# A new list of steps for a one-core kernel that mixes a state-space layer with linear attention

## The chip, the cores and the metric

The kernel runs on one core of a Trainium2 chip. A core has a matrix engine (TensorE; PE in the profile, its weight loads PEld), a vector engine (VectorE; DVE), a scalar engine (ScalarE; ACT), GpSimd (POOL) and a sync engine (SyncE; SP) that here only issues DMAs. Each engine has its own queue of instructions and takes them in the order in which the program lists them; between engines, semaphores hold an instruction back until its data is there. The metric is the device time of one execution in microseconds (us), the median of several runs.

## The reference, cut to what matters

`x` is 2048 tokens of 512 features in bf16. Two branches read it, and a sigmoid gate mixes them:

```python
g = sigmoid((x * gate_w).sum(-1, keepdims=True))
# branch A: a complex diagonal recurrence over 2048 time steps
Lam_bar = exp(dt * Lam);  B_bar = ((Lam_bar - 1) / Lam)[:, None] * Bmat
Bu = einsum("bld,pd->blp", x, B_bar)
for t in range(L):  h = Lam_bar * h + Bu[:, t, :]
a = 2 * einsum("blp,dp->bld", hseq, Cmat).real + x * Dskip
# branch B: linear attention, 32 heads of 16, softmax(+p) and softmax(-p) as features
q, k, v = split(x @ wqkv);  pq, pk = q @ w_phi, k @ w_phi
phi = concat([softmax(p), softmax(-p)])          # for q and for k
kv = einsum("bhsf,bhsd->bhfd", phi_k, v);  z = phi_k.sum over s
o = (phi_q @ kv) / (phi_q @ z + 1e-6);  b = o @ wo
return g * a + (1 - g) * b
```

## The kernel before

All of `x` is held transposed in SBUF (`xT`), as 16 blocks of 128 tokens, regrouped so that tokens with the same remainder modulo 8 stand together. Branch B computes keys (steps `k0` to `k15`), values (`v0` to `v15`) and queries (`q0` to `q15`), each four matmuls into one PSUM bank and a copy out of it; features by maximum, minimum, exponential and sum (`x`, `n`, `e`, `s` with the number of a key group; `X`, `N`, `E`, `S` with the number of a query group of four blocks); and the sum of keys times values (`a`). Branch A makes the inputs of the recurrence for 8 groups of 64 complex states (`b` and `g` with group and part), runs a scan over every eighth step (`z0`, `z1`, each for half of the groups), and fills in the steps between (`sa`, `sb`, `H`, then `hd`, `hk`, `ek` on ACT, DVE and DMA and `dp` on PE). The output of block n is gathered in one PSUM bank: `yn` (branch A), `tn` (branch B times `wo`), with `on` making the normalized attention rows before that.

All of this is written as Python generators, one per step name, each yielding after a few instructions of one engine. The string `ORDER` lists the names; each time a name comes, its generator advances by one part:

```python
for tok in ORDER.split():
    tok, _, banks = tok.partition("@")
    tok, _, eng = tok.partition(":")
    sel["eng"] = "dve" if eng == "D" else "act"
    sel["banks"] = [int(b) for b in banks]
    next(st[tok])
```

So `ORDER` decides four things: the sequence of every engine's queue (program order is queue order), the PSUM bank that a step uses (`@3`: bank 3; `o` takes the named bank and the next one, as pairs), whether a copy out of PSUM or a scaling goes to DVE (`:D`) or to ACT, and the sequence of the DMAs. Nothing is planned at run time. Below, "part 2 of `z0`" means its third yield, counted from zero.

Parts that matter below:

- Loads on SP: `Lk` (two halves of the key weights), `Lx` (two plain loads of blocks 0 and 1, then seven DMA transposes of two blocks each, line 236; the last three bring blocks 10/11, 12/13 and 14/15), `Lv` (value weights), `Lq` (two DMA transposes of the query weights, line 249), `Lb` (two plain loads of `A_B_re` and `A_B_im`, line 241, then four DMA transposes to `BT`, line 244), `Lc` (four transposes of C, line 255), `Lo` (`wo`), `Ld` (the row `Dskip`, then two loads of 256 KB of `x` for the blocks whose skip term is added by DVE, line 272). Key block n needs its `Lx`; the query weights `w0` to `w3` need both `Lq`; `b` and `g` need `BT`.
- Other DMAs on SP: `C` (line 698), `XX0`, `XX1` (swapped halves of the states, line 774), the last two parts of each `S` (feature transposes, line 620), `O` (transposes of a pair of `on` rows, line 904, which `t` needs), `R` (output, line 932). A DMA that has to wait holds up everything behind it in SP's queue.
- `Z`: a matmul on zeros, sixteen of them at the head. `W`, `T`: PE transposes of weights and of blocks 0 and 1, each with a copy. `f0` to `f3`: the folded key weights.
- `a4` adds the last key group; `Y` (four parts on DVE, lines 829 and 831) masks the finished sums into `KVm`; every `o` reads `KVm`.
- `sb1`, `H2`, `H3`: one PE part and then an addition on DVE (line 735).
- part 3 of `on` is the normalization on DVE (line 891), which also frees the two banks of `on`.
- part 0 of a feature sum (`S1`: line 566, `sm<-EE`) reads what both exponentials of that group (line 589) have written.
- part 3 of `ekm` is the last addition on DVE for states of group m (line 806); part 0 of `y10` reads groups 0 to 3.

Of the kernel before, what the change touches and what calls it, by code (L numbers as in the profile page):

```python
# [23 lines left out]
ORDER = """
Z@0 Lk Lk Z Z Z B Z Z B Z Z Z Lx Z Z W01@2 Z W00@3 Z B Z W00 Z B W01 W10@1 W00 Lx B W10:D W11@4 Lx W01 Z f0@2 f1@5
T1@1 W11 T0@4 f0:D f1 Lv T1 f2@3 f3@0 Lx Lx T0:D f2 V@2 V k1@5 P k0@4 f3:D P Lx P2 P k0 P2 P2 U P2 k1 P2 U P3 P4 k0
k1 U k2@2 P3 P4 k3@1 n0 v0@5 P4 x0 k5@6 k2 v1@2 Lb Lq n0 i x0 P2 k7@0 v3@4 i V2@3 k3 x0 v0 k5 i n0 i k9@1 x0 v1 i i
Lq x0 n0 Lb k7 M n0 k8@7 k4@0 M k6@2 n1 M Lx w2@6 x1 w0@5 V2 v6@3 x0z Lx n1 x1 v3 n1 L Da Lx Lb Lb x1 Lb Da Lb e0 n1
k4 w3@4 k6 k9 w3 x1 w0 x1 v6 k10@0 n1 k10 s0 x2 k11@2 s0 w1@4 k8 M2 e1 k13@1 k15@3 w1 Db x2 k15 b11@7 U x2 b10@5 k11
b01@0 b20@4 n2 x2 Lc n2 b10 x2 n2 s0 w2 n2 M2 s0 k13 b00@3 n2 M2 g01@5 Da Db x3 g10@1 b30@6 s0 b01 b20 s0 Lc e2 Db  # L30
s1 b31@4 g10 g30@0 n3 b30 s0 c1:D x3 b00 g00@3 s1 g30 k12@6 c0:D b31 g00 g01 k14@2 e2 b11 a0@74 g00 gw a0 g01 g10 n3
q1@1 s1 b21@3 n3 x3 s1 Da s1 x3 g30 v2@0 c0:D k12 n3 s1 q3@6 k14 q0@2 g01 s2 x3 n3 s2 q1 q1 b21 Lc c0:D q2@3 n4
g11@1 x4 e3 g11 g11 q3 v2 g31@0 g01 s1 x4 q3 g20@6 g31 q0 q0 a1 q2 n4 s2 x4 e3 g31 g20 c0 g11 g01 n4 c2 g01 g31 a1
g01 g20 s2 g21@2 x4 q2 g11 s3 Lc g21 c2 g21 g11 s2 v5@3 g01 g21 c1 v5 g31 g21 s2 x4 v4@6 g21 s3 c2:D g31 s3 b40@3
g01 g11 v4 g21 n4 s3 g31 g21 s3 g31 v7@5 b50@6 b40 g21 g31 n4 g11 s2 q6@3 X0 N0 G0 c1 g21 s2 X0 g11 a2 q4@2 c2 g31
q7@0 c1 g11 q6 N0 b50 z0@6 c3 Lo z0 b70@1 v7 a2 q4 s3 z0 q4 q5@5 q7 a2 e4 q6 s3 q7 b70 q5 X0 e4 N0 z0 a2 c3 X0 b71@3
z0 g40@6 X0 b61@1 N0 z0@0 b71 g50@2 b61 g50 g50 q5 z0 z0 b51@5 X1 c3 v10@0 g40 s4 b60@3 z0 sa0@2 g70@1 b51 g61@5 N0
X1 b60 g71@3 s4 g71 g70 v10 g51@0 c3 sa0 X1 g40 sb0@2 Ld s4 s3 N1 g60@6 sb0 N1 s4 g51 g61 g51 N1 E0 E0 C g60 C g70
g51 S0 v11@2 s4 G1 N1 G0 v8@1 g60 Ld S0 g51 H1@6 g61 v11 s4 v8 X1 S0 b41@2 v9@1 g51 H1 S0 s4 hd1 C g51 s4 a3 S0 g71
v9 g41@6 a3 b41 g41 H0@2 g41 a3 a3 hd1 G0 g71 g51 C S0 g71 g61 g41 G1 S0 g71 g61 H0 g41 XX0 g41 q9@2 g61 g71 hd0 G1  # L40
g51 g51 g61 g71 g41 g61 q10@1 X1 g61 XX0 g41 N1 q9 g71 g41 g61 q8@0 g71 g41 S0 hd1 z1@6 q8 q10 z1 S0 z1 q11@3 q9 q11
v13@6 z1 q10 E1 q8 E1 z1 v12@0 XX0 z1@1 X2 N2 v14@2 q14@5 v13 q11 v12 z1 z1 X2 XX0 v15@1 N2 q12@3 z1 v15 hd0 v14 S0
S0 N2 hd1 hd1 hd0 hd1 q14 S1 a4 N2 S1 X2 sa1@0 a4 S1 sa1 a4 q12 a4 sb1@6 S1 q13@0 Y Y sb1 S1 hd0 q15@7 Y X2 H2@6 Y
o0@1 q14 G2 S1 END q15 X2 XX1 y1@5 q15 hd0 q13 q12 S1 o0 o1@3 H3@7 N2 y1 H3 o1 H2 hd0 o3@6 XX1 XX1 o0 q13 o0 o1 E2
E2 o1 N3 S1 XX1 y3@0 hk4 S1 o2@1 y2@4 y0@3 y2 O0 o2 y0 S1 y0 S2 o3 X3 o2 hk6 y1 o3 hk4 hk7 o2 t1 t0 y3 o3 hk7 hk6
y4@1 y2 S2 hk4 hk5 O1 t0 S2 o5@6 X3 S2 y3 hk4 hk7 S2 N3 t1 X3 S1 o4@2 S2 y6@5 hk5 X3 t2 S2 o5 ek0 hk5 hk7 R0 S2 o4
o5 o4 ek0 t3 hk5 hk6 t2 o4 ek3 ek3 o5 t3 o6@2 S2 N3 S2 hk6 X3 N3 o6 o7@6 y5@4 ek0 o7 o6 N3 o6 O2 o7 o7 ek2 ek1 y5 y4
y6 S2 dp5@0 ek1 y4 ek3 y5 dp6@2 o8@6 dp6 dp5 y6 E3 t4 ek2 Ld o9@2 o8 ek0 y7@0 o9 y7 ek2 ek1 o8 t5 o8 o9 ek2 o9 ek1
ek4:D E3 o10@6 t4 y7 o10 O3 o11@2 ek5 S3 t7 ek3 o10 t6 ek6 o11 ek4 o11 O4 y10@1 o10 S3 G2 dp1@6 ek5:D y11@7 t6 t7 t5
o11 ek5 S3 O5 ek7 ek6 ek4 ek5 ek7 S3 dp0@2 ek6 R2 ek7 ek4 y9@0 ek6 ek7 S3 dp7@4 y8@3 dp2@5 S3 dp2 y10 y8 dp3@5 t8  # L50
y11 S3 R1 S3 dp7 dp4@4 G2 dp1 u8 S3 S3 S3 t11 t8 G3 dp0 t10 y9 t9 o13@2 dp3 o13 o12@5 o12 u9 dp4 t9 R3 y14@4 y12@0
u10 o12 G3 y14 o12 o13 o15@5 o13 o15 y12 o15 o14@2 t10 o14 G3 y12 o14 u11 o15 y13@1 O6 y13 t11 y15@56 y15 y13 t12
t13 R4 R5 o14 O7 y14 t14 O8 t12 t13 R6 y15 t14:D R7 t15 t15 t15 R8 t15:D R8
"""
# [946 lines left out]
```

## Time and profile before

| | before |
|---|---|
| median of 3 runs | 151.49 us (151.43 to 152.28) |
| the profiled execution | 151.96 us, of which 150.2 us are the span from first to last instruction |
| granted TensorE clock | 0.996 |
| HBM read and written | 3.56 MB, 2.10 MB |
| DMA traffic in all | 19.73 MB, 131 GB/s on average |

The profile shows for each engine its busy time and its share of the span, and gives idle time to the event that ended it. A timeline line reads: start, duration, engine, source line, operation, output<-input, and in brackets the idle time before it and what ended that. Durations of neighbouring instructions overlap by 0.06 to 0.2 us, since an engine starts one before the last has drained; so the distance from start to start is the true price of a line, and the chain of waits prints such distances.

### The profile page before, as it was taken

The page shows a single profiled execution, that of the slowest core. Times are in us where ns is not written, and L with a number is a line of the kernel's source. Part 1 is how long each engine was busy: PE and PEld are TensorE (multiplying, and loading weights), DVE is VectorE, ACT ScalarE, POOL GpSimd, SP SyncE. Part 2 cuts the span into 40 slices and gives each one's busy share as a digit, 9 for nine tenths or more (in the row PEclk, how much of TensorE's full clock was granted, in tenths as well). Part 3 has the DMA queues.
Part 4 walks back from the last instruction along what each step waited for, and adds up shares of the span by engine and source line. Part 5 has one row for each costly group of instructions (what it writes and reads, how often), then busy time and mean ns, then how long its engine had stood idle before and what let it go on. Part 6 is the DMA issues. An engine that isn't in the chain of part 4 may idle for free.

```text
span 150.2 us, 2835 instructions
## 1 busy us (share of the span) xinstructions
PE 140.9 (94%) x986; PEld 75.2 (50%) x986; DVE 135.1 (90%) x332; ACT 121.9 (81%) x241; POOL 21.4 (14%) x47
## 2 busy tenths in 40 slices
...
GB/s 120 237 265 178 143 230 232 166 180 238 20 0 0 0 0 4 2 0 105 244 74 94 183 142 70 175 186 181 229 181 166 156 65 212 128 214 77 201 82 72
DMA packets 54110, 19.73 MB, mean 131 GB/s; under 512 B 44496, under 2 KB 54096, under 8 KB 54096
## 3 DMA queue, kind: packets, MB, share of 16 engines
...
q8 instruction: 7, 0.11, 0.3%
q14 instruction: 7, 0.06, 0.2%
HBM read 3.56 MB, written 2.10 MB: 38 GB/s over the span
## 4 chain that ended last, share of the span: by engine, by line
PE 55%; DVE 24%; SPq 10%; DMA 7%; issue 1%; ACT 0%; DVEq 0%
PE PS L516 12%; PE PS L860 9%; PE PS L648 9%; PE PS L643 9%; PE PS L916 6%; SPq L236 5%; DMA xT<-in_A_x_dram 4%; DVE on L891 3%; DVE sm L566 3%; SPq L249 3%; DMA oT<-on 3%; PE PS L660 2%; DVE EE L577 2%; DVE EE L616 2%; DVE HH L735 2%; DVE EE L583 2%
## 5 line engine op out<-in xcount | busy, mean ns | idle before, releaser
L516 PE MATMUL PS<-WKV,xT 128*128 128x480 bf16 (+1 forms) x128 | 29.6, 373 | 1.7 <-DMA xT<-in_A_x_dram 1.7
L589 ACT ACTIVATE EE<-EE 128x2048 bf16<-128x2048 bf16 x16 | 30.7, 1944 | 0.0
L516 PEld LDWEIGHTS <-xT 128*128 128x128 bf16 x192 | 18.3, 99 | 20.0 <-DMA xT<-in_A_x_dram 1.8
L860 PE MATMUL PS<-C,LS 128*128 128x512 bf16 (+1 forms) x104 | 23.0, 363 | 0.0
L135 ACT CAST Xq<-PS 128x480 bf16<-128x480 f32 x32 | 17.6, 584 | 1.7 <-PE PS L516 1.7
L916 PE MATMUL PS<-Wo,oT 128*128 128x512 bf16 (+2 forms) x68 | 15.6, 367 | 0.3 <-DMA oT<-on 0.3
L643 PE MATMUL PS<-xT,BT 128*128 128x512 bf16 x64 | 15.7, 379 | 0.0
L648 PE MATMUL PS<-xT,BT 128*128 128x512 bf16 x64 | 15.6, 379 | 0.0
L516 PE MATMUL PS<-Wq,xT 128*128 128x481 bf16 x64 | 15.0, 367 | 0.0
L135 ACT CAST LS<-PS 128x512 bf16<-128x512 f32 x24 | 14.1, 630 | 0.9 <-PE PS L648 0.7
L860 PEld LDWEIGHTS <-LS 128*128 128x128 bf16 x104 | 9.5, 98 | 9.7
L684 POOL DMA_DIRECT2D LS<-CT x4 | 4.9, 1226 | 62.2 <-ACT HH L135 49.6
L922 ACT ACTIVATE ot<-PS,G 128x512 bf16<-128x512 f32 (+1 forms) x11 | 7.2, 670 | 5.8 <-PE PS L916 5.7
L882 ACT ACTIVATE ld<-PS 128x32 f32<-128x32 f32 x16 | 2.8, 197 | 10.2 <-PE PS L877 7.6
L465 ACT ACTIVATE CT<-HH,dgs 128x512 bf16<-128x512 bf16 x15 | 10.7, 718 | 0.2 <-DVE HH L735 0.2
L891 DVE TENSOR_TENSOR on<-PS,rd 128x512 bf16<-128x512 f32 x16 | 10.8, 710 | 0.0
L577 DVE TENSOR_TENSOR EE<-Xq,mx 128x2048 bf16<-128x2048 bf16 (+1 forms) x9 | 10.0, 1107 | 0.8 <-PE PS L633 0.8
L465 ACT ACTIVATE CT<-CS,nsn 128x512 bf16<-128x512 bf16 x15 | 10.5, 725 | 0.0
L583 DVE TENSOR_TENSOR EE<-mn,Xq 128x2048 bf16<-128x2048 bf16 (+1 forms) x9 | 10.0, 1112 | 0.0
L566 DVE TENSOR_TENSOR sm<-EE 128x2048 bf16<-128x2048 bf16 (+1 forms) x9 | 10.0, 1107 | 0.0
L135 ACT CAST vx<-PS 128x512 bf16<-128x512 f32 x16 | 9.9, 633 | 0.1
L604 DVE TENSOR_TENSOR EE<-EE,rc 128x2048 bf16<-128x2048 bf16 x8 | 9.7, 1219 | 0.1
...
## 6 DMA issues: line engine op xcount, KB each, us to landing
...
```

Source lines behind the costliest of these rows:

```text
L135: nc.scalar.copy(out=out_ap, in_=in_ap)
L465: nc.scalar.mul(out=out_ap, in_=in_ap, mul=s_)
L516: MM(out=pt[:], lhsT=xT[:, kt, ti * P:(ti + 1) * P], rhs=W[:, kt, 0:pt.shape[-1]], start=(kt == 0), stop=(kt == KT - 1))
L566: VT(out=dst, in0=cur[:, :, :, 0:n, :], in1=cur[:, :, :, n:2 * n, :], op=op)
L577: VT(out=half(EE, 0), in0=X5, in1=live["mx", p].to_broadcast([P, L, 8, Dh, 4]), op=ALU.subtract)
L583: VT(out=half(live["EE", p], 1), in0=live["mn", p].to_broadcast([P, L, 8, Dh, 4]), in1=X5, op=ALU.subtract)
L589: aexp(out=EE[:, l_:l_ + 2], in_=EE[:, l_:l_ + 2], func=ACT.Exp)
L643: MM(out=pt[:], lhsT=BT[:, m, kt, :], rhs=cells(kt, r), start=(kt == 0), stop=False, skip_group_check=True)
L648: MM(out=pb[:], lhsT=BT[:, m, kt, :], rhs=cells(kt, 2 * pr), start=(kt == 0), stop=(kt == KT - 1))
L860: MM(out=py[:], lhsT=hs[m], rhs=C2[:, m, c:c + w], start=(m == 0), stop=False)
L891: VT(out=live["on", g_][:, u], in0=pn[:, :, :, 0:Dh], in1=rd[:].unsqueeze(3).to_broadcast([P, 2, 16, Dh]), op=ALU.mult)
L916: MM(out=py[:], lhsT=oT[:, g, :], rhs=Wo[:, g, c:c + w], start=False, stop=(g == HG - 1))
```

## The change

Only the string `ORDER` is replaced. Both lists have 897 entries, and every step comes as often as before: the same instructions are issued, in another sequence, with other banks, and a few on the other of the two engines that can do them. The head of both lists, the stretch about `a4` and `Y`, and the one about `y10`:

```diff
-Z@0 Lk Lk Z Z Z B Z Z B Z Z Z Lx Z Z W01@2 Z W00@3 Z B Z W00 Z B W01 W10@1 W00 Lx B W10:D W11@4 Lx W01 Z f0@2 f1@5
-T1@1 W11 T0@4 f0:D f1 Lv T1 f2@3 f3@0 Lx Lx T0:D f2 V@2 V k1@5 P k0@4 f3:D P Lx P2 P k0 P2 P2 U P2 k1 P2 U P3 P4 k0
...
-v13@6 z1 q10 E1 q8 E1 z1 v12@0 XX0 z1@1 X2 N2 v14@2 q14@5 v13 q11 v12 z1 z1 X2 XX0 v15@1 N2 q12@3 z1 v15 hd0 v14 S0
-S0 N2 hd1 hd1 hd0 hd1 q14 S1 a4 N2 S1 X2 sa1@0 a4 S1 sa1 a4 q12 a4 sb1@6 S1 q13@0 Y Y sb1 S1 hd0 q15@7 Y X2 H2@6 Y
-o0@1 q14 G2 S1 END q15 X2 XX1 y1@5 q15 hd0 q13 q12 S1 o0 o1@3 H3@7 N2 y1 H3 o1 H2 hd0 o3@6 XX1 XX1 o0 q13 o0 o1 E2
...
-y6 S2 dp5@0 ek1 y4 ek3 y5 dp6@2 o8@6 dp6 dp5 y6 E3 t4 ek2 Ld o9@2 o8 ek0 y7@0 o9 y7 ek2 ek1 o8 t5 o8 o9 ek2 o9 ek1
-ek4:D E3 o10@6 t4 y7 o10 O3 o11@2 ek5 S3 t7 ek3 o10 t6 ek6 o11 ek4 o11 O4 y10@1 o10 S3 G2 dp1@6 ek5:D y11@7 t6 t7 t5
...
+Lk Z@0 Z Z B Z Z Z Z Z Z Z Z W00@3 B Z Z Lk W01@2 Lx Z Z B W00 B W00 W01 Lx B T0@4 W01:D W11@1 Lx T0 T1@3 Lx T1:D
+W10@5 Lv Lx f1@4 W11 Lx V@2 f0@1 W10 V f1 f2@3 f3@2 f0:D P P P2 P2 f2 k1@5 f3 P2 k0@4 Z Lq Lb P2 P k0 U P2 k1 k0 P4
...
+v14@1 q8 z1 q11 q9 z1 X2 v15@2 E1 q11 XX0 E1 hd0 S0 XX0 z1 N2 z1@5 X2 v13@6 z1 z1 hd0 X2 S0 v12@3 v14 q12@5 XX0 v12
+v13 q14@1 z1 sa1@3 a4 v15 a4 S1 a4 q12 a4 hd1 q13 N2 S1 X2 S1 sa1 sb1@6 N2 Y q12 XX0 hd0 hd0 Y Y Y hd1 S1 N2 sb1 q14
+o0@2 END o1@4 y1@0 X2 q13 S1 H2@6 o0 y1 o1 hd0 o1 hd1 hd1 H2 hk4 q15@7 H3@6 q14 q15 N2 H3 XX1 o0 o0 E2 y3@1 XX1 S1
...
+dp5@2 ek3 o7 o7 N3 y4 y7@3 O2 o7 ek2 y7 dp5 o9@5 dp6 G2 ek1 E3 o8@1 y7 t4 y6 ek0 ek1 S2 ek3 o9 o8 ek2 o9 o8 t5 E3 o8
+O3 o9 dp4@1 o10@5 t4 ek1 o10 ek2 ek3 y10@2 o10 ek4:D O4 ek5:D ek4 y11@0 ek4 o10 S3 t6 ek5:D o11@5 ek6 ek7 t7 t6 ek5
...
```

SP's queue, read out of the two lists (name and count of the part, from zero):

```text
before: Lk.0 Lk.1 Lx.0 Lx.1 Lx.2 Lv Lx.3 Lx.4 Lx.5 Lb.0 Lq.0 Lq.1 Lb.1 Lx.6 Lx.7 Lx.8 Lb.2 Lb.3 Lb.4 Lb.5 Lc.0-3 Lo Ld.0
        C.0 C.1 Ld.1 C.2 C.3 XX0.0-3 S0.9 S0.10 XX1.0-3 O0 S1.9 O1 S1.10 R0 S2.9 O2 S2.10 Ld.2 O3 O4 O5 R2 R1
        S3.9 S3.10 R3 O6 R4 R5 O7 O8 R6 R7 R8
after:  Lk.0 Lk.1 Lx.0 Lx.1 Lx.2 Lx.3 Lv Lx.4 Lx.5 Lq.0 Lb.0 Lq.1 Lx.6 Lb.1 Lx.7 Lx.8 Lb.2 Lb.3 Lc.0 Lo Lc.1 Lb.4 Lc.2 Lb.5 Lc.3
        Ld.0 Ld.1 Ld.2 C.0-3 XX0.0 S0.9 XX0.1 S0.10 XX0.2 XX0.3 XX1.0-3 O0 S1.9 O1 S1.10 R0 S2.9 O2 S2.10 O3 O4 R1 O5 R2 R3
        S3.9 S3.10 R4 O6 O7 O8 R5 R6 R7 R8
```

On PE, about the same places: before, `k10 k11 w1 k13 k15 b11` with `k12` and `k14` later, and after, `w1 k11 k10 k13 k14 k15 g00` with `k12` later; before, `a4 sa1 a4 a4 a4 sb1 q13 q15 H2 o0 y1 o1 H3 y1 o3`, and after, `sa1 a4 a4 a4 a4 sb1 o0 o1 y1 H2 y1 q15 H3 y3 y1 o2`, with `q13` moved ahead of the last values (part 2 of each `q` on DVE as well); before, `t5 o10 y7 o11 t7 t6 y10`, and after, `t5 dp4 o10 y10 y11 t6 o11 t7`. The copies that change engine: `W01`, `T1`, part 1 of `c1` and of `c2`, part 9 of `g01`, part 7 of `g21`, part 0 of `ek5` and the 384-column half of `t15` go from ACT to DVE; `W10`, `T0`, `f3`, part 2 of `c0` and the 128-column half of `t15` go from DVE to ACT. On POOL, part 2 of `hd0` now stands ahead of part 2 of `hd1`.

More of the change, by code (lines that the diff above doesn't have):

```diff
@@ L24 @@
 ORDER = """
-Z@0 Lk Lk Z Z Z B Z Z B Z Z Z Lx Z Z W01@2 Z W00@3 Z B Z W00 Z B W01 W10@1 W00 Lx B W10:D W11@4 Lx W01 Z f0@2 f1@5
-T1@1 W11 T0@4 f0:D f1 Lv T1 f2@3 f3@0 Lx Lx T0:D f2 V@2 V k1@5 P k0@4 f3:D P Lx P2 P k0 P2 P2 U P2 k1 P2 U P3 P4 k0
-k1 U k2@2 P3 P4 k3@1 n0 v0@5 P4 x0 k5@6 k2 v1@2 Lb Lq n0 i x0 P2 k7@0 v3@4 i V2@3 k3 x0 v0 k5 i n0 i k9@1 x0 v1 i i
-Lq x0 n0 Lb k7 M n0 k8@7 k4@0 M k6@2 n1 M Lx w2@6 x1 w0@5 V2 v6@3 x0z Lx n1 x1 v3 n1 L Da Lx Lb Lb x1 Lb Da Lb e0 n1
-k4 w3@4 k6 k9 w3 x1 w0 x1 v6 k10@0 n1 k10 s0 x2 k11@2 s0 w1@4 k8 M2 e1 k13@1 k15@3 w1 Db x2 k15 b11@7 U x2 b10@5 k11
@@ L30 @@
[L30 to L39, printed above, removed]
@@ L40 @@
-v9 g41@6 a3 b41 g41 H0@2 g41 a3 a3 hd1 G0 g71 g51 C S0 g71 g61 g41 G1 S0 g71 g61 H0 g41 XX0 g41 q9@2 g61 g71 hd0 G1
-g51 g51 g61 g71 g41 g61 q10@1 X1 g61 XX0 g41 N1 q9 g71 g41 g61 q8@0 g71 g41 S0 hd1 z1@6 q8 q10 z1 S0 z1 q11@3 q9 q11
-v13@6 z1 q10 E1 q8 E1 z1 v12@0 XX0 z1@1 X2 N2 v14@2 q14@5 v13 q11 v12 z1 z1 X2 XX0 v15@1 N2 q12@3 z1 v15 hd0 v14 S0
-S0 N2 hd1 hd1 hd0 hd1 q14 S1 a4 N2 S1 X2 sa1@0 a4 S1 sa1 a4 q12 a4 sb1@6 S1 q13@0 Y Y sb1 S1 hd0 q15@7 Y X2 H2@6 Y
-o0@1 q14 G2 S1 END q15 X2 XX1 y1@5 q15 hd0 q13 q12 S1 o0 o1@3 H3@7 N2 y1 H3 o1 H2 hd0 o3@6 XX1 XX1 o0 q13 o0 o1 E2
@@ L45 @@
-E2 o1 N3 S1 XX1 y3@0 hk4 S1 o2@1 y2@4 y0@3 y2 O0 o2 y0 S1 y0 S2 o3 X3 o2 hk6 y1 o3 hk4 hk7 o2 t1 t0 y3 o3 hk7 hk6
-y4@1 y2 S2 hk4 hk5 O1 t0 S2 o5@6 X3 S2 y3 hk4 hk7 S2 N3 t1 X3 S1 o4@2 S2 y6@5 hk5 X3 t2 S2 o5 ek0 hk5 hk7 R0 S2 o4
-o5 o4 ek0 t3 hk5 hk6 t2 o4 ek3 ek3 o5 t3 o6@2 S2 N3 S2 hk6 X3 N3 o6 o7@6 y5@4 ek0 o7 o6 N3 o6 O2 o7 o7 ek2 ek1 y5 y4
-y6 S2 dp5@0 ek1 y4 ek3 y5 dp6@2 o8@6 dp6 dp5 y6 E3 t4 ek2 Ld o9@2 o8 ek0 y7@0 o9 y7 ek2 ek1 o8 t5 o8 o9 ek2 o9 ek1
-ek4:D E3 o10@6 t4 y7 o10 O3 o11@2 ek5 S3 t7 ek3 o10 t6 ek6 o11 ek4 o11 O4 y10@1 o10 S3 G2 dp1@6 ek5:D y11@7 t6 t7 t5
@@ L50 @@
[L50 to L53, printed above, removed]
+Lk Z@0 Z Z B Z Z Z Z Z Z Z Z W00@3 B Z Z Lk W01@2 Lx Z Z B W00 B W00 W01 Lx B T0@4 W01:D W11@1 Lx T0 T1@3 Lx T1:D
@@ new lines @@
+W10@5 Lv Lx f1@4 W11 Lx V@2 f0@1 W10 V f1 f2@3 f3@2 f0:D P P P2 P2 f2 k1@5 f3 P2 k0@4 Z Lq Lb P2 P k0 U P2 k1 k0 P4
+k3@1 P4 P4 P3 k2@2 k5@6 k7@0 i k1 P3 x0 i n0 Lq V2@3 i k2 k6@2 v0@5 i x0 k3 Lx Lb n0 x0 k5 x0 P2 i v1@6 x0 M n0 n0
+k6 i k8@7 x1 Lx k4@2 k7 n0 M L n1 x0z U M e0 k8 n1 v3@4 k9@1 V2 Lx w3@3 k9 M2 k4 v6@7 Da w0@1 x1 x1 n1 x1 x1 Lb w2@2
+v1 w3 w1@0 Lb M2 n1 s0 s0 n1 v6 s0 Da k11@6 Lc x2 Lo Db w2 k10@3 Lc k13@2 n2 s0 n2 k14@7 w1 n2 k15@0 v3 w0 g00@1 x2
+k10 b01@3 b00@4 e1 x2 s0 k11 n2 Lb gw Lc k14 v0 x2 k13 U x2 n2 x3 s0 U b30@6 b01 b00 b10@5 n3 k15 Db x3 s0 n3 g11@3
@@ new lines @@
+b11@7 a0@04 s1 x3 g00 M2 Lb b30 s1 x3 n3 e2 b10 Db c1:D b21@6 a0 Da k12@2 b11 s1 g11 n3 s1 g10@7 g30@5 e2 b21 g10 x3
+g00 k12 b20@6 s1 Da n3 c1:D n4 g10 Lc b31@2 q1@1 b20 g11 g01@6 c0:D s1 e3 g30 g01 s1 g11 c0:D n4 s2 x4 b31 q1 g01
+v2@7 s2 n4 s2 g20@2 g01 g30 x4 s2 q1 v2 g11 e3 g01 a1 g01 g11 q3@7 s3 g20 s2 g20 v4@5 g31@1 s2 q3 g11 Ld x4 g01 q0@2
+s3 g01 c0 q0 g31 q3 g31 g01 s2 v5@7 a1 g01:D q2@6 g11 s3 n4 v4 c3 x4 v5 g31 g21@5 g11 c1 g21 g31 v7@7 s3 g11 g21 x4
+q2 v7 b40@3 q0 n4 s3 g31 s2 v10@7 s3 g21 g31 b40 N0 X0 b61@2 q5@3 g31 q2 N0 g21 e4 c0 g21 q6@6 a2 b61 X0 v10 q6 c2
@@ new lines @@
+N0 a2 s3 X0 s3 q4@2 q4 a2 g21 c2:D a2 q6 G0 q7@7 q5 g21:D g21 X0 g31 g21 g31 b50@6 X0 b70@1 N0 z0@5 q4 q7 z0 g40@2
+q7 N0 g50@7 z0 b50 c3 e4 c2:D g50 q5 X1 z0 G0 b51@5 b60@3 g50 g60@6 s4 z0 b70 b71@1 z0@7 E0 N1 s4 Ld z0 g40 z0 b51
+s4 z0 Ld g51@5 s4 b60 g60 g61@7 g40 c3 c2 sa0@2 g51 g70@3 g60 X1 sa0 g61 sb0@2 E0 g51 c3 c1 b71 sb0 s4 g71@6 S0 g70
+g51 C g70 v8@1 g61 s4 g51 H1@3 N1 v11@2 v8 S0 g61 g61 g71 H1 g71 G0 g61 g51 b41@3 v9@1 S0 v11 g71 s4 H0@2 b41 g71
+hd1 a3 S0 S0 g41@3 s4 S0 G1 g61 H0 X1 v9 g71 g41 S0 g41 N1 g41 G1 g71 S0 a3 a3 a3 G1 g41 g71 g71 hd0 g51 g51 g61 X1
```

8 lines of the change are left out of this document (added).

## The prediction

> **What bounds the kernel now.** I read the busy times and the shares of the chain that ended last first, then the busy time by stretch, then the table of who waited for whom.
>
> ```profile
> span 150.2 us, 2835 instructions
> PE 140.9 (94%) x986; PEld 75.2 (50%) x986; DVE 135.1 (90%) x332; ACT 121.9 (81%) x241; POOL 21.4 (14%) x47
> ...
> PE 55%; DVE 24%; SPq 10%; DMA 7%; issue 1%; ACT 0%; DVEq 0%
> ```
>
> ```profile
> 27.00:79.00 52.00, 52.00 (x332) 26.33 (x330) 50.69 (x107) 50.29 (x97) 2.30 (x5) 1.00 0.32 73
> 79.00:98.00 19.00, 17.39 (x156) 9.90 (x155) 18.98 (x46) 18.47 (x42) 4.67 (x4) 1.00 0.76 135
> 98.00:115.00 17.00, 16.78 (x133) 9.04 (x132) 17.00 (x37) 17.00 (x35) 0.00 (x0) 1.00 1.05 186
> ```
>
> ```profile
> PE PS L516 <- DMA xT<-in_A_x_dram: 1.7, 1, 1.7
> PE PS L877 <- DVE HH L735: 0.8, 1, 0.8
> PE PS L633 <- ACT vx L135: 0.7, 1, 0.7
> PE PS L916 <- DMA oT<-on: 0.3, 1, 0.3
> ```
>
> The columns of the second view are length, then busy time of PE, weight loads, DVE, ACT and POOL, then clock, DMA share and rate. PE never stops from 27 to 79. From 79 to 115 DVE never stops (35.98 of 36 us) and ACT hardly. So three queues are full at once, and what a new order can win is what PE waits: 1.7 + 0.8 + 0.7 + 0.3 = 3.5 us in four places. If all of it went and nothing came in its place, the median of 151.49 would fall to 148.0; that is the floor. Outside these places a new order can only hold its ground or lose.
>
> The work itself is the same: sixteen warming matmuls in both lists, every matmul, load and activation kept. So I go from wait to wait, and ask in each stretch what the new order does to it. The profiled execution took 151.96 us, 1.76 more than its span; the sum is made against that and then moved to the median, 0.47 below.
>
> **The head, up to 27 us.** The rows of SP's and PE's timelines, the landings of the transposes issued at 18.6 and 21.3, and two pieces of the chain:
>
> ```profile
> 15.32 0.60 SPq L241 DMA_DIRECT2D C<-in_A_B_im_dram  x1
> 15.97 6.69 SPq L236 DMA_TRANSPOSE xT<-in_A_x_dram  x3
> ```
> ```profile
> 15.97 6.56 DMA xT<-in_A_x_dram
> ...
> 37.36 0.81 PE PS L516 x4
> ```
> ```profile
> L236 SPq DMA_TRANSPOSE xT<-in_A_x_dram x1: 2727/2727/2727, 18.6 to 18.6; - x1
> ...
> DMA to landing us min/median/max: 5.3/5.3/5.3
> ```
> ```profile
> L236 SPq DMA_TRANSPOSE xT<-in_A_x_dram x1: 1315/1315/1315, 21.3 to 21.3; - x1
> ...
> DMA to landing us min/median/max: 3.6/3.6/3.6
> ```
> ```profile
> 22.57 1.79 PE L516 MATMUL PS<-WKV,xT 128*128 128x480 bf16 x8 [1.65 <-DMA xT<-in_A_x_dram]
> ...
> 26.03 1.24 PE L648 MATMUL PS<-xT,BT 128*128 128x512 bf16 x5
> ```
>
> PE runs dry at 20.92 and waits 1.65 us for blocks 10/11, which land at 15.97 + 6.56 = 22.53. Blocks 12/13 land at 18.6 + 5.3 = 23.9, blocks 14/15 at 21.3 + 3.6 = 24.9. The change puts this load ahead of the load of B_im, so it is issued at 15.3; the other two keep their places behind the same work and land as before. With the B_im load no longer in front, I let blocks 10/11 land at about 21.2: 22.53 less the distance of 1.3 us between the landings of 10/11 and 12/13, the nearest row for what one more transfer in front costs. PE reaches them at 20.92 + 0.2 (`w1` is now ahead) = 21.1, so this wait goes. But after `k11` and `k10` (0.81 us each) PE stands at 22.8 and waits 1.1 us for blocks 12/13; after `k13` at 24.7 it waits 0.2 us for 14/15; after `k14` and `k15` it is 26.5. Before, PE was at 26.03 with the same keys done but `k14`, whose 0.81 us it paid at 37.36. That makes 26.84 against 26.5. So of 1.65 us **0.3** is won; the rest is paid two keys later, because the last load ends where it ended. The bounds are 0 and 1.65.
>
> The Trainium skill, page "DMA: Bandwidth & Descriptors", section "Queues, rings and completion order", says that on each DMA engine the descriptors of one issuing queue are consumed in ring order. The trace agrees in that these loads land in the order of issue (22.5, 23.9, 24.9). By that rule the gain stands at 0.3; if queued loads shared the engines instead, blocks 10/11 would still land at 22.5 and the gain would be 0.
>
> B_im is issued some 2.6 us later, and the transposes behind it read it: had it landed after 22.7, SP would stand there, and behind it the rest of `Lb`, `Lc` and `Lo`. I take that the two swapped loads are both in by 22.5, as now, and cost it at nothing; the cover is the wait for blocks 14/15. If it is gone, `g00` starts up to 1.0 late. The reshuffled `W`, `T`, `f`, and the `Z` that now stands between `k0`'s halves, put the first keys 0.2 us later at most; the wait for loads behind them hides it.
>
> **27 to 79 us.** PE has no wait here, so there is nothing to win, and every step that is moved can lose. I compared the place of each producer and each consumer by the work ahead of it in its queue. The tight pairs are copies out of banks between 50 and 57 us: the scan inputs' copies on ACT come late against PE's `b40`, `v10` and `b61`.
>
> ```profile
> L135 ACT CAST LS<-PS 128x512 bf16<-128x512 f32 x24 | 14.1, 630 | 0.9 <-PE PS L648 0.7 <-PE PS L660 0.2
> L465 ACT ACTIVATE CT<-CT,csp 128x1024 bf16<-128x1024 bf16 x2 | 2.4, 1200 | 0.0
> L467 DVE TENSOR_SCALAR CS<-CT,csp 128x512 bf16<-128x512 bf16 x3 | 1.0, 348 | 0.0
> ```
>
> ACT gains part 2 of `c0` (1.2 us there) and loses two scalings of half that width, which DVE takes at 0.35 each. ACT has idled 0.9 us for PE in this group before, and most of that goes when keys come earlier, so I expect it in time: **0**, with +0.9 (one copy and a half of 0.63) as the far end. Below nothing is excluded, as PE is full. `Ld.1` and `Ld.2` go ahead of `C`, right behind `Ld.0`; they wait there for the last keys, and behind them in SP's queue stands only `C`, which needs a sum that comes much later.
>
> **79 to 98 us, values to the first attention rows.** From the timelines of PE and ACT and the chain:
>
> ```profile
> 90.66 0.67 PE L633 MATMUL PS<-vx,EE 128*128 128x68 bf16 x16 [0.67 <-ACT vx L135]
> 91.31 0.40 PE L750 MATMUL PS<-HH,dg 128*128 128x128 bf16 x4
> 91.55 1.79 PE L516 MATMUL PS<-Wq,xT 128*128 128x481 bf16 x8
> 93.18 0.38 PE L758 MATMUL PS<-HH,dg 128*128 128x256 bf16 x2
> ```
> ```profile
> 97.14 0.42 PE L877 MATMUL PS<-KVm,phT 128*128 128x68 bf16 x8 [0.81 <-DVE HH L735]
> ```
> ```profile
> 84.35 3.71 ACT L589 ACTIVATE EE<-EE 128x2048 bf16<-128x2048 bf16 x2
> ```
> ```profile
> 86.96 0.34 DVE mn L566
> ...
> 87.95 0.12 DVE mn L566
> ...
> 88.09 1.23 DVE sm L566
> ...
> 91.51 0.33 DVE KVm L829
> 91.84 0.19 DVE KVm L831
> ...
> 93.49 1.13 DVE EE L577
> ...
> 95.78 1.30 DVE HH L735 x2
> ...
> 97.15 1.20 DVE on L891 x2
> ```
>
> Removed: `q13` (0.81) and `sa1` (0.24) now stand ahead of `a4`, so `a4` comes 1.05 us later against ACT's value copies, and its wait of 0.67 is covered. Added: before, `q13`, `q15` and `H2` (91.55 to 93.40, 1.85 us) filled PE while DVE made `KVm`; now `o0` follows `sb1` at once. `Y` takes 2 x (0.33 + 0.19) = 1.04, and one `q` part of 0.13 stands within it: from 91.31 that is 92.48, while PE is free at 91.55. So PE waits 0.93 at `o0`. Then `o2` shares its banks with `o0`, whose normalization stands behind two subtractions (2 x 1.13), three additions (3 x 0.65) and some 0.64 of small parts, and takes 0.60: 92.48 + 5.45 = 97.93. PE's work up to there is `o0`, `o1` (0.25 each), three halves of `y` (0.86 each), `q15`, `H2`, `H3` and a skip term (0.81 + 3 x 0.22): 4.55, to 97.03. So it waits 0.90 again, where the wait of 0.81 was. Sum: 0.93 + 0.90 - 0.67 - 0.81 = **+0.35**. On DVE, two parts of `N2` (0.34 and 0.12) leave the place ahead of `S1`'s first part, which reads what the exponentials leave at 84.35 + 3.71 = 88.06; it started at 88.09 as it was, so DVE could stand 0.46 there. I count it as filled, since DVE has two scalings of 0.35 more ahead of that; if not, +0.46.
>
> **98 to 134 us.**
>
> ```profile
> 115.14 0.76 SPq L272 DMA_DIRECT2D WKV<-in_A_x_dram  x1
> ```
> ```profile
> 120.46 0.47 DVE L806 TENSOR_TENSOR LS<-CT 128x512 bf16<-128x512 bf16 x1
> ```
> ```profile
> 121.98 1.03 PE L860 MATMUL PS<-C,LS 128*128 128x512 bf16 x4
> ```
>
> `Ld.2` stood in front of the `oT` transpose that PE awaited for 0.3 us; gone, that transpose is issued 0.8 earlier, and the wait with it: -0.3. What is late next is `y10`: it passes `o11`, `t7` and `t6` and lets one `dp4` in (2.0 - 0.2 us earlier, so about 120.0 with PE's gains), while `ek3`'s last addition, done at 120.93, passes a sum of 1.13 and a scaling of 0.27: 119.5. That is 0.5 in hand by the rows, and less than nothing if DVE stood at `S1`. I count +0.1, with 0 and +0.6 as ends. Sum **-0.2**.
>
> **The tail.** The last part of the last feature sum has one `dp` addition (0.65) more ahead of it on DVE, so its transposes land that much later; but PE now does both halves of `y13` and `y14` (four times 0.86) among `o12` to `o14`, where it did three. The last output halves swap engines: **0**, from -0.1 to +0.5.
>
> **The sum**: -0.3 + 0 + 0.35 - 0.2 + 0 = -0.15 on 151.96, so 151.8 for an execution like the profiled one, and **151.35** for the median.
>
> **The rivals.** *Slower: DVE loses its step at the exponentials.* The first part of `S1` waits 0.46, everything behind it on DVE goes with it, `o0` and `o2` wait that much more (twice: PE pays once, DVE again at `y10`, 0.6), and the copies of 50 to 57 us cost 0.9 on PE: 151.35 + 0.46 + 0.5 + 0.9 = 153.2. It decides once ACT ends the exponentials later than 88.06. For it: DVE is full from 79 to 115, so nothing lost there is found again. Against it: PE has waits there which take a part of it up. Chance 0.22.
>
> *Faster: the waits go, and none comes.* If PE's work runs ahead of DVE by the gain in the head and DVE's order lets `Y` and the normalization through in time, 0.81 + 0.67 + 0.3 + 0.3 = 2.1 go: 149.4. It needs `o0` not to wait for `KVm`, and the rows put 1.85 us of cover away from there. Chance 0.13.
>
> *The loads do not come earlier.* Blocks 10/11 land at 22.5 still, or B_im comes later than 22.7 and `BT` with it: +0.3 to +1.0, so 151.7 to 152.4. For it: what SP's transposes take to issue (1.3 when free, 2.7 at 18.6) shows a queue already full. Chance 0.15.
>
> **How the numbers follow.** The forecast has 0.50. A change of 1%, 1.5 us, is about what a measurement of this kernel can tell from none: below 150.0 or above 153.0. Of the fast rival about 0.11 lies below 150.0; of the slow one and the tails of the others about 0.22 above 153.0; the rest, 0.67, is within. The range reaches down by about half of the fast rival's gain, to 150.2, and up to the slow rival, 153.2.
>
> **What would show it.** Right: a PE wait of about 1.1 us at `k13`, none at `k11`; `a4` without a wait; PE waits of about 0.9 at `o0` (for `KVm`) and at `o2` (for `on`); no wait for `oT` near 120. Wrong: a PE wait between 27 and 79 of over 0.3 in all; SP standing at line 244; a DVE gap before the sum at about 88; `y10` waiting for line 806. If PE waits under 2.5 us in all, the fast rival holds.

## The result, and the profile after

| | before | after |
|---|---|---|
| median of 17 runs each, same chip | 151.59 us (151.38 to 152.37) | 151.10 us (150.76 to 151.44) |
| ratio | | 0.9960, 95% interval 0.9948 to 0.9973 |
| profiled execution | 151.96 us, span 150.2 | 151.44 us, span 149.6 |
| PE ends its last matmul | 146.10 us | 145.46 us |

The change gains 0.4%, some 0.6 us. The busy times and shares of the page of the changed kernel:

```profile
span 149.6 us, 2829 instructions
PE 140.5 (94%) x972; PEld 75.3 (50%) x986; DVE 136.2 (91%) x335; ACT 121.8 (81%) x238; POOL 21.7 (15%) x47
```

The counts differ by matmul records that this trace lacks (972 for 986 weight loads), so PE's busy time can't be compared to tenths. Busy time by stretch, columns as before:

```profile
27.00:79.00 52.00, 50.90 (x313) 25.62 (x316) 51.56 (x105) 49.98 (x95) 3.33 (x5) 1.00 0.34 73
79.00:98.00 19.00, 17.84 (x158) 10.38 (x159) 18.77 (x48) 18.09 (x39) 4.95 (x4) 1.00 0.77 137
98.00:115.00 17.00, 16.68 (x131) 9.03 (x134) 17.00 (x38) 16.97 (x38) 0.00 (x0) 1.00 1.12 194
```

PE now stops between 27 and 79, where it never had, and DVE a little between 79 and 98. Who waited for whom, PE's rows: total, times, longest:

```profile
PE PS L336 <- DVE Drow L156: 1.2, 1, 1.2
PE PS L633 <- ACT EE L589: 0.7, 1, 0.7
PE PS L877 <- DVE on L891: 0.6, 1, 0.6
PE PS L877 <- DVE KVm L831: 0.5, 2, 0.3
PE PS L877 <- DVE LS L735: 0.3, 1, 0.3
```

The first row stands before 2 us and is in both kernels. Of the old four places (blocks 10/11, `a4`, `o2`, `oT`) three are gone and `o2` waits less; `a0` and `o0` are new. `o8` had waited too, 0.22 for DVE at 114.84, which the four places left out; now it waits 0.34. Their places on PE's timeline, and the start of the first keys (8.09 us before):

```profile
8.94 0.97 PE L516 MATMUL PS<-WKV,xT 128*128 128x480 bf16 x4 [0.19 <-DVE WKV L137]
...
21.97 4.21 PE L516 MATMUL PS<-WKV,xT 128*128 128x480 bf16 x20
26.02 1.03 PE L643 MATMUL PS<-xT,BT 128*128 128x512 bf16 x4
...
32.92 0.43 PE L633 MATMUL PS<-vx,EE 128*128 128x68 bf16 x8 [0.69 <-ACT EE L589]
...
43.49 0.38 PE L670 MATMUL PS<-HH,dg 128*128 128x256 bf16 x2
44.01 0.42 PE L633 MATMUL PS<-vx,EE 128*128 128x68 bf16 x8
...
90.49 1.20 PE L633 MATMUL PS<-vx,EE 128*128 128x68 bf16 x32
...
92.45 0.29 PE L877 MATMUL PS<-KVm,phT 128*128 128x68 bf16 x4 [0.31 <-DVE KVm L831]
92.93 0.54 PE L877 MATMUL PS<-KVm,phT 128*128 128x68 bf16 x12 [0.19 <-DVE KVm L831]
...
98.16 0.41 PE L877 MATMUL PS<-KVm,phT 128*128 128x68 bf16 x8 [0.62 <-DVE on L891]
...
116.67 0.41 PE L877 MATMUL PS<-KVm,phT 128*128 128x68 bf16 x8 [0.34 <-DVE LS L735]
```

Two things to read here. From 21.97 twenty key matmuls run without a stop, so neither blocks 10/11 nor those behind them are waited for, and the features of branch A start at 26.02. And at 43.49 two short matmuls are followed by `a1` only 0.52 us later (in the run with `a0` moved, the same step needs 0.22): a stop of 0.30 without a bracket, for a value copy that ACT ends at 43.97. The wait at 32.92 is put down to ACT; by DVE's timeline it is a scaling (line 604) that ends at 32.86. From start to start it costs 0.86, not 0.69: the four matmuls ahead start at 31.20 and take 0.22 each.

Lists in another order can't be compared by the clock alone. So I use PE's **lead**: the start of a step's first matmul, minus the time by which the profiled kernel before had done as much matmul work as the list has ahead of that step. Negative is ahead; matmul work that an experiment adds counts as work, so the difference at the end is free of it. It is worked out from the starts of the 986 weight loads (990 where four matmuls are added), one execution per kernel:

```text
                     g00     q9     t0     t5     t6    end
                   ~26 us  ~79   ~103   ~118   ~121   ~146   time ratio to before
after              -0.80  +0.49  +0.11  +0.01  -0.65  -0.64  0.9960
head_loads_back    +0.76  +0.88  +0.52  +0.42  -0.24  -0.22  0.9964
a0_later           -0.19  -0.07  +0.34  -0.25  -0.92  -0.91  0.9939
pe_twice_45        +0.15  +0.15  -0.08  -0.19  -0.85  -0.82  1.0017
dve_twice_84       +0.36  +0.48  +0.83  +0.72  +0.06  +0.07  0.9999
y0_ahead_of_o2     +0.21  +0.33  -0.31  -0.08  -0.75  -0.73  0.9952
waits_filled       +0.41  +0.53  -0.14  -0.52  -0.59  -0.56  0.9948
after_ld_late      -0.39  +0.56  +0.21  +0.10  -0.57  -0.56  0.9957
q13_behind_sb1     +0.09  +0.49  +0.14  +0.02  -0.64  -0.63  0.9921
x_blocks_first     +0.52  +0.45  +0.07  -0.03  -0.69  -0.68  0.9951
a0_and_q13         +0.20  +0.63  +0.27  +0.17  -0.49  -0.48  0.9929
before_ld_early    +0.59  +0.59  +0.57  +0.58  +0.08  +0.11  0.9992
before_loads_sw.   +0.37  +0.38  +0.36  +0.37  -0.12  -0.09  0.9948
```

The first figure can be read from rows that are shown: the list before has done all but `k14` at 26.03, where its features start, so 26.03 + 0.81 = 26.84 stands against 26.02, 0.82 ahead. Against the matmuls' own starts the columns from `q9` to `t5` come out 0.1 to 0.2 lower for the rows of the new list, so small differences between columns mean little. The rows of one list belong together.

In the old list (last two rows) what the head gives or costs is carried to `t5` unchanged. In the new list it isn't: heads from -0.80 to +0.52 all stand between +0.33 and +0.56 at `q9` where `a0` keeps its place and no work is added ahead, while the later head of +0.76 stands at +0.88. The changed kernel gives back 1.29 us between 26 and 79. From `t5` to `t6` every new list gains about 0.66 (only `waits_filled`, which has `o8` elsewhere, does not), or 0.49 by the matmuls' own starts. Both rows of the old list gain 0.5 there too: this is a stop of 0.48 in the profiled kernel before, which the other two profiles of the old list don't have (see "Near 120 us").

### The profile page after: what moved, and what is told of

It reads as the page before. It is cut to its first block, busy times and chain, and to the rows that moved or that the text cites. A ratio compares the mean times of both kernels' runs of the same rounds, so it can differ in the third digit from the quotient of the medians.

```text
span 149.6 us, 2829 instructions
## 1 busy us (share of the span) xinstructions
PE 140.5 (94%) x972; PEld 75.3 (50%) x986; DVE 136.2 (91%) x335; ACT 121.8 (81%) x238; POOL 21.7 (15%) x47
## 5 line engine op out<-in xcount | busy, mean ns | idle before, releaser
L516 PE MATMUL PS<-WKV,xT 128*128 128x480 bf16 (+1 forms) x124 | 28.9, 372 | 0.5 <-DVE WKV L137 0.2
L135 ACT CAST Xq<-PS 128x480 bf16<-128x480 f32 x32 | 18.2, 595 | 0.9 <-PE PS L516 0.8
L465 ACT ACTIVATE CT<-HH,dgs 128x512 bf16<-128x512 bf16 x14 | 9.8, 718 | 0.2 <-DVE HH L735 0.2
L648 PEld LDWEIGHTS <-BT 128*128 128x128 bf16 x64 | 6.3, 99 | 7.1
```

Source lines behind the costliest of these rows:

```text
L135: nc.scalar.copy(out=out_ap, in_=in_ap)
L465: nc.scalar.mul(out=out_ap, in_=in_ap, mul=s_)
L516: MM(out=pt[:], lhsT=xT[:, kt, ti * P:(ti + 1) * P], rhs=W[:, kt, 0:pt.shape[-1]], start=(kt == 0), stop=(kt == KT - 1))
L648: MM(out=pb[:], lhsT=BT[:, m, kt, :], rhs=cells(kt, 2 * pr), start=(kt == 0), stop=(kt == KT - 1))
```

## The experiments

Each was timed in five rounds. Kernels sent together shared a chip and its runs of the kernel before, whose median was 152.18, 152.11, 152.42 and 152.07 on these, so ratios are compared, not times. The changed kernel was not timed again beside them; its 0.9960 is that of the result. The intervals are +-0.0018 to +-0.0030.

**Where the head's time goes.** The new list with its loads in the old order (SP's queue):

```diff
-Lx.5 Lq.0 Lb.0 Lq.1 Lx.6 Lb.1 Lx.7 Lx.8
+Lx.5 Lb.0 Lq.0 Lq.1 Lb.1 Lx.6 Lx.7 Lx.8
```

> The new list with the loads of the head in the old order (B_re, both query weights, B_im, then blocks 10/11). PE theory (what PE gains early is kept to the end): blocks 10/11 land near 22.5 instead of 20.1, PE waits 1 us or more before k11, and the 0.3 to 0.8 us that the head won are lost: 151.4 to 151.9 us. DVE theory (DVE sets the pace from 79 us on, PE's lead is taken back in waits at o0 and o2): the wait before k11 comes too, but the waits at o0 and o2 (1.1 us) shrink by as much: 151.0 to 151.2 us.

0.9964 (0.9946 to 0.9982). PE's timeline of this kernel:

```profile
23.53 4.22 PE L516 MATMUL PS<-WKV,xT 128*128 128x480 bf16 x20 [1.46 <-ACT Wq L135]
27.59 1.03 PE L643 MATMUL PS<-xT,BT 128*128 128x512 bf16 x4
```

Blocks 10/11 land at 23.48, PE waits until 23.53 (the releaser named had long been done), and the features start 1.57 later than in the changed kernel. But the wait at `a0` is gone, so PE ends only 0.42 later, and the ratio doesn't move beyond its interval.

The old list with the new order of loads:

```diff
-Lb.0 Lq.0 Lq.1 Lb.1 Lx.6 Lx.7
+Lq.0 Lb.0 Lq.1 Lx.6 Lb.1 Lx.7
```

> The kernel before with nothing of the change but its order of the loads in the head (Lq.0 ahead of Lb.0, and blocks 10/11 ahead of B_im). By the prediction's step the wait of 1.65 us at blocks 10/11 goes, and PE, which reads blocks 12/13 and 14/15 later in this list, has its feature matmuls 0.3 us earlier: a ratio of 0.998. If the head is set by VectorE's and ScalarE's chain of features rather than by these loads: the wait goes and comes back ahead of the first attention rows, ratio 1.000 within 0.001. If PE alone set the time: 1.65 us won, 0.989.

0.9948 (0.9925 to 0.9971): some 0.8 us, where 0.3 was expected. The one trace doesn't show that gain. Blocks 10/11 land at 20.78, but their wait is replaced by one of 1.02 for blocks 12/13 and one of 0.69 for the query weights, and PE is 0.37 behind until `t5`; it ends 0.09 earlier only because it doesn't meet the stop at `t7` (see "Near 120 us"). So ratio and trace disagree, and whether the swap alone helps the old list stays open, as does whether it adds to the rest in the new one.

Blocks 12/13 ahead of B_im too, in the new list:

```diff
-Lx.6 Lb.1 Lx.7 Lx.8
+Lx.6 Lx.7 Lb.1 Lx.8
```

> The changed kernel with the load of blocks 12/13 ahead of that of B_im too. The prediction's step says that the wait of k13 for blocks 12/13 (0.7 to 1.5 us in the runs so far, none in the profile of the changed kernel) is what the shortened wait of k11 turned into, and that B_im has no room to come later. By that: k13 does not wait, B_im lands 1.2 later, SP stands before the transposes of BT that much longer, and the first feature matmul g00 waits up to 1.0 for BT; the time is the same or up to 0.5 us longer (0.996 to 0.9995). If BT had room: k13's wait goes, nothing comes for it, and PE reaches g00 at 26.0 or before: 0.5 us shorter (0.992).

0.9951 (0.9924 to 0.9977), no different from the changed kernel. PE's timeline:

```profile
25.20 1.79 PE L516 MATMUL PS<-WKV,xT 128*128 128x480 bf16 x8 [0.64 <-DMA xT<-in_A_x_dram]
27.15 1.04 PE L643 MATMUL PS<-xT,BT 128*128 128x512 bf16 x4 [0.15 <-ACT lg L597]
```

12/13 land at 21.66, so `k13` doesn't wait; the wait is now at `k14`, for 14/15 at 25.15. B_im lands at 24.36 and the first part of `BT` at 27.10, 0.05 before `g00`: the room for B_im is used up, at a cost of 0.15 by the bracket and 0.3 by the starts (eight matmuls of 0.20 from 25.20 would let the next step start at 26.82), not 1.0. Whatever the order, the last block lands at 24.2 to 25.8, and in eleven of the thirteen other profiles PE waits for one of the last three loads; only the changed kernel's own and that of `after_ld_late` show no such wait.

The first `a0` behind `b21`, in the new list:

```diff
-b11@7 a0@04 s1
...
-b21@6 a0 Da
+b11@7 s1
...
+b21@6 a0@04 a0 Da
```

> The new list with the first part of a0 moved on PE from behind b11 to behind b21, 1.1 us of matmuls later. Both theories: its wait of 0.7 us for the scaled exponentials at 32.9 us goes. PE theory: 0.5 to 0.7 us less, 150.4 to 150.6 us. DVE theory: the waits at o0 and o2 grow from 1.1 to some 1.7 us and the time stays at 151.0 to 151.2 us.

0.9939 (0.9913 to 0.9964). PE's timeline:

```profile
24.06 0.98 PE L516 MATMUL PS<-WKV,xT 128*128 128x480 bf16 x4 [0.85 <-DMA xT<-in_A_x_dram]
...
103.83 1.90 PE L916 MATMUL PS<-Wo,oT 128*128 128x512 bf16 x8 [0.56 <-DMA oT<-on]
```

The wait at `a0` is gone, and PE nearly keeps its lead as far as `q9` (-0.19 to -0.07). Then part of it turns into a wait for `oT` at `t0`, which the changed kernel didn't have.

**Which queue sets the time behind.** The four value matmuls of `v4` (45 us) done twice, and the first maximum of `X2` (85 us) done twice:

```diff
-        tile_mm(pv, KO[ti], Wv)
+        for _ in range(2 if ti == 4 else 1):
+            tile_mm(pv, KO[ti], Wv)
```

> The new list with the four matmuls of v4 done twice (near 45 us), 0.86 us more on PE and nothing else. PE theory: 0.8 to 0.9 us more, 151.9 to 152.0 us. DVE theory: the waits of PE at o0, o2 and o8 (1.5 us) take it up: 151.1 to 151.4 us.

```diff
-            VT(out=dst, in0=cur[:, :, :, 0:n, :], in1=cur[:, :, :, n:2 * n, :], op=op)
+            for _ in range(2 if key == ("mx", "G2") and n == Dh // 2 else 1):
+                VT(out=dst, in0=cur[:, :, :, 0:n, :], in1=cur[:, :, :, n:2 * n, :], op=op)
```

> The new list with the first maximum of X2 done twice (near 85 us), 0.60 us more on DVE and nothing else. PE theory: 0 to 0.2 us more, 151.1 to 151.3 us. DVE theory: 0.5 to 0.6 us more, 151.6 to 151.7 us, with the waits of PE at o0 and o2 longer by as much in sum.

1.0017 (0.9987 to 1.0047) and 0.9999 (0.9979 to 1.0019): against the changed kernel +0.0057 and +0.0039, or 0.86 and 0.59 us, each give or take some 0.4. In the traces PE ends 0.67 and 0.71 later. DVE's timeline of the second (its line numbers are one higher from there on):

```profile
84.92 1.41 DVE L567 TENSOR_TENSOR mx<-Xq 128x1024 bf16<-128x1024 bf16 x2
```

and what PE waits for there:

```profile
87.05 0.28 PE L724 MATMUL PS<-w,Sw 128*128 128x256 bf16 x1 [0.29 <-DVE w L721]
...
92.45 0.40 PE L751 MATMUL PS<-HH,dg 128*128 128x128 bf16 x4 [0.50 <-DVE HH L736]
```

The pair takes 1.41 where one took 0.68, and all of it reaches PE, at `sb1` and before: `sb1` starts at 92.45 instead of 91.75. Both additions are paid nearly in full, so work added to PE at 45 us or to DVE at 85 us finds no room. Other places were not tried.

**Waits given work.** `y0` ahead of `o2`; then this with `a0` behind `b21` and `o8` behind `y7` and `y6`:

```diff
-XX1 y1 o2@2 o1 XX1 y0@6 O0
+XX1 y1 y0@6 o2@2 o1 XX1 O0
```

> The changed kernel with the first half of y0 (four matmuls, 0.86 us) put ahead of o2, so that the 0.62 us that PE waits at o2 for the normalization of o0 has work in it. If PE's waits are what is left to win from 98 us on: the wait at o2 goes, PE is 0.6 earlier from there to its end, and the ratio to the kernel before falls from 0.996 to 0.992. If PE and VectorE are tied there (as the two doubled pieces of work were both paid): o2 starts without a wait, but the same 0.6 comes back as a wait of PE for VectorE within the next 20 us, PE's end moves by less than 0.2, and the ratio stays at 0.995 to 0.997.

```diff
-E3 o8@1 y7 t4 y6 ek0
+E3 y7 y6 o8@1 t4 ek0
```

> The changed kernel with three of its PE waits given work: the first a0 behind b21 (0.69 us at 32.9), the first half of y0 ahead of o2 (0.62 at 98.2), o8 behind y6 and y7 (0.34 at 116.7). If PE alone set the time all three would be gained: 1.65 us, a ratio of 0.985. If PE and VectorE are tied from some 45 us on, only what lies before that can be gained, which is the first of the three: 0.993 to 0.995, as with that move alone (0.994), and new PE waits for VectorE take the place of the other two.

0.9952 (0.9927 to 0.9977) and 0.9948 (0.9921 to 0.9975). PE's, DVE's and ACT's timelines with `y0` moved, and then those of the changed kernel:

```profile
103.23 1.89 PE L916 MATMUL PS<-Wo,oT 128*128 128x512 bf16 x8
...
105.82 0.67 PE L877 MATMUL PS<-KVm,phT 128*128 128x68 bf16 x16
106.63 1.02 PE L860 MATMUL PS<-C,LS 128*128 128x512 bf16 x3
...
103.27 0.68 DVE L566 TENSOR_TENSOR sm<-sm 128x1024 bf16<-128x1024 bf16 x1
...
105.90 0.68 ACT L922 ACTIVATE ot<-PS,G 128x512 bf16<-128x512 f32 x1
```
```profile
103.65 1.89 PE L916 MATMUL PS<-Wo,oT 128*128 128x512 bf16 x8
...
106.24 0.67 PE L877 MATMUL PS<-KVm,phT 128*128 128x68 bf16 x16
106.75 1.02 PE L860 MATMUL PS<-C,LS 128*128 128x512 bf16 x3
...
103.36 0.68 DVE L566 TENSOR_TENSOR sm<-sm 128x1024 bf16<-128x1024 bf16 x1
...
105.97 0.68 ACT L922 ACTIVATE ot<-PS,G 128x512 bf16<-128x512 f32 x1
```

The wait at `o2` is gone and PE reaches `t0` 0.42 earlier, but DVE only 0.09. Three microseconds on, the rows of attention take 0.81 to the next step instead of 0.51, without a bracket, and 0.12 is left. That step is `y4`, in the bank that `y1` had, and ACT empties this bank until 106.58 (line 922), only 0.07 earlier than in the changed kernel. So the filled wait comes back as a wait for a queue that was not moved. With all three filled, 1.65 us by the brackets, the time is that of the changed kernel within the interval, which leaves room for some 0.6 us of them.

`q13` back behind `sb1`:

```diff
-C q13@7 N1
...
-a4 hd1 q13 N2 S1 X2 S1 sa1 sb1@6 N2
...
-Y Y Y hd1 S1
+C N1
...
+a4 hd1 N2 S1 X2 S1 sa1 sb1@6 q13@7 N2
...
+Y Y Y hd1 q13 S1
```

> The changed kernel with q13 (0.81 us of PE) put back behind sb1, so that it stands again between a4 and o0. By the prediction's own step the change traded a wait of 0.67 at a4 for one at o0: put back, a4 waits for ScalarE's value copies again, 0.5 to 0.8, and the wait of o0 for KVm (0.31 + 0.19 in the changed kernel) goes; the two cancel within 0.3 us and the ratio stays at 0.995 to 0.998. If q13's new place is a gain (a4's wait covered, o0's half matmuls hidden), the time goes up by 0.5: 0.9995.

0.9921 (0.9896 to 0.9947), though PE's end is the same within 0.01. The wait for ACT's value copies comes back (0.30, at `q14`) with one of 0.4 for DVE at the scan of the states; those at `o0` are gone. With `a0` moved as well:

> The changed kernel with the two single moves that came out best: the first a0 behind b21, and q13 back behind sb1. If what a0's move won (0.3 us at PE's end) and what q13's move does (nothing at PE's end, though its ratio was 0.992) stand by themselves: PE ends 0.9 us before the kernel before, as with a0's move alone, and the ratio is 0.992 to 0.995. If both ratios are real and add up (0.994 and 0.992 against 0.996 of the changed kernel): 0.990. If PE and VectorE are tied, the gain at a0 is given back by 118 us, and the ratio is 0.996.

0.9929 (0.9903 to 0.9955). Nothing shows that the two add: its trace has PE's end no earlier (-0.48), and with `a0` moved PE waits at `a1` for the value copy instead, 0.16 at 44.16. Both ratios lie below the changed kernel's 0.9960. The interval of `q13` alone ends at 0.9947, just below where the changed kernel's begins (0.9948), but this was on another chip and no trace shows a reason, so I call them no worse, not better.

**Near 120 us.** `Ld.2` back in front of `O3` in the new list, and `Ld.2` behind `Ld.1` in the old:

```diff
-z0 Ld g51@5
...
-o8 O3
+z0 g51@5
...
+o8 Ld O3
```

> The changed kernel with Ld.2 (a load of 0.76 us on SP's queue) back in front of the transpose O3, as in the old list. If the gain near 120 us is Ld.2's leaving (the prediction's step): O3 lands 0.8 later, PE waits about 0.3 at t6, and the time goes up by 0.3 us (a ratio of 0.998 to the kernel before). If it is that t6 and t7 stand behind more work now: O3 has the cover of that work, no wait for oT comes, and the time is that of the changed kernel within 0.1 us (0.996).

```diff
-g60 Ld S0
...
-ek2 Ld o9@2
+g60 Ld Ld S0
...
+ek2 o9@2
```

> The kernel before with Ld.2 behind Ld.1 in SP's queue, and nothing else of the change. If Ld.2 in front of O3 made PE wait: O3 lands 0.8 us earlier, the wait of 0.3 for oT near 120 goes, and the ratio is 0.998. If PE and VectorE are tied there, the wait goes and comes back as one for VectorE at y10 or at the o steps: 1.000, within 0.001.

0.9957 (0.9931 to 0.9983) and 0.9992 (0.9964 to 1.002). SP's and PE's timelines of the new list with `Ld.2` late:

```profile
116.66 0.58 SPq L272 DMA_DIRECT2D WKV<-in_A_x_dram  x1
117.33 3.21 SPq L904 DMA_TRANSPOSE oT<-on  x2
```
```profile
121.38 1.03 PE L916 MATMUL PS<-Wo,oT 128*128 128x512 bf16 x4
```

`O3` lands at 117.33 + 3.4 = 120.8, and `t6` starts behind other work at 121.38 all the same. And of the old list, as it was and with `Ld.2` early:

```profile
119.50 0.42 PE L877 MATMUL PS<-KVm,phT 128*128 128x68 bf16 x8
120.24 1.04 PE L916 MATMUL PS<-Wo,oT 128*128 128x512 bf16 x4 [0.32 <-DMA oT<-on]
```
```profile
120.08 0.42 PE L877 MATMUL PS<-KVm,phT 128*128 128x68 bf16 x8
120.34 1.89 PE L916 MATMUL PS<-Wo,oT 128*128 128x512 bf16 x7
```

With `Ld.2` early the wait is gone: from start to start 0.26 instead of 0.74, so the stop was worth 0.48, more than its bracket. (In the old list `t7` stands first of the pair.) But the old list with only the head's loads swapped, where `Ld.2` still goes out in front of `O3`, doesn't have the stop either:

```profile
119.87 0.42 PE L877 MATMUL PS<-KVm,phT 128*128 128x68 bf16 x8
120.13 1.89 PE L916 MATMUL PS<-Wo,oT 128*128 128x512 bf16 x7
```

There `O3` is issued at 116.15 and lands 3.7 later, at 119.85, in time for 120.13. In the profiled kernel before it is issued at 115.99 and lands 4.2 later, at 120.19, and PE had come to the pair 0.37 sooner. So this stop is not in every execution of the old list. Moving `Ld.2` is enough to rule it out (in the old list `O3` then lands at 118.76), and so is `t6` behind more work; the new list has both. But one profile of the kernel before doesn't show that the stop is there as a rule, nor how much of it is `Ld.2`, and whether the old list gains by the move, its ratio leaves open.

## Why the prediction was right

The time was forecast at 151.35 and came at 151.10, within 1%. But the steps erred both ways, and by lead their sizes are -0.80, +1.29, -0.38 and -0.75 where -0.3, 0, +0.35 and -0.2 stood.

- **Blocks 10/11.** Right. Forecast to land at 21.2, they came at 20.1 to 21.1 in ten executions. The Trainium skill, page "DMA: Bandwidth & Descriptors", section "Queues, rings and completion order", has an issuing queue's descriptors consumed in ring order on each engine; the trace agrees, as the swapped loads swapped their landings (10/11 at 20.07 and B_im at 22.54, and with the old order B_im at 22.75 and 10/11 at 23.48). The wait moved on to `k13`: 0.5 to 1.5 in eight of them, none in the profile of the changed kernel and in `after_ld_late`, where 12/13 came early (23.3 and 23.8). The head starts its features 0.45 earlier on average (the old order of loads: 0, +0.59 and +0.76; the new one in the new list, nine executions: 0.00) where 0.3 was forecast; the profiled execution, at -0.80, was an early one. The first keys start 0.85 later, not 0.2, and PE comes to `k11` at 21.97 instead of 21.1. A wait behind hides most of that, as said: at 21.1 PE would have waited at `k13` for blocks 12/13, which landed at 23.34.
- **B_im.** Right: it landed at 22.54, its transposes followed at 22.64, and nothing waited for `BT`. The price if that cover went was put at up to 1.0; `x_blocks_first` used the room up and showed 0.15 to 0.3.
- **27 to 79, counted 0.** This step failed, and the sign named for it, over 0.3 us of waits here, came. `b40`, `v10` and `b61` don't wait, but I had looked for tight pairs only there. `a0` waits 0.69 for DVE's feature scaling (0.86 by the starts) and `a1` 0.30 for a value copy, together 1.16 of the 1.29 and more than the +0.9 of the far end, which was counted for other copies. That the features set the pace there, and take back what the head gives beyond them, is how I read the leads at `q9`.
- **79 to 98, +0.35.** The mechanism was right, the terms were mis-sized. `a4` doesn't wait (90.49), the sum at 88 starts behind other work (88.38 us) with no gap on DVE. But `o0` waits 0.31 + 0.19 and not 0.93, since its first four matmuls need only the half of `KVm` that is done first, and `o2` 0.62 and not 0.90. With 0.67 and 0.81 gone this makes -0.36; the lead says -0.38, but is itself good only to 0.1 or 0.2.
- **98 to 134, -0.2.** Right in sign: the wait for `oT` went, and `y10` didn't come late. It was worth 0.48 in the profiled kernel before, not 0.3, as I took the bracket for the whole loss. That `Ld.2` alone made it isn't shown: the new list doesn't wait with `Ld.2` late, and another profile of the old list with `Ld.2` in its old place has no stop either. The remaining 0.27 I can't assign to a step.
- **The tail, 0.** Right: from `t6` to the end the lead moves by 0.01.
- **The rivals.** The slower one's first condition, a late sum at 88, did not come; the faster one's mark did and its time didn't: from 20 us on PE's brackets fall from 3.7 to 2.3, under the 2.5 that I had named, but the time by only 0.6. Brackets are no time, as the filled waits show. That the loads don't come earlier is refuted by their landings.

The forecast was near by luck: two misses of opposite sign cancelled, 0.8 too good up to 79 us, 1.3 too bad behind.
